# The last attention batch of a two-stage mixture-of-experts kernel: its chunk and transposes before the first ranks, two copies before a tile's root, and filler products in one batch instead of four

## The chip, the core and the metric

The kernel runs on one core of a Trainium2 chip. The core has TensorE (PE, the matrix engine, with its weight load PEld), VectorE (DVE), ScalarE (ACT), GpSimd (POOL) and SyncE (SP, which here only issues transfers), each with its own queue worked off in order. The metric is the device time of one execution in microseconds (us); less is better.

## What is computed

Attention without softmax (the keys' and values' 64x64 product per head, then the queries times it, then a root-mean-square norm), then two mixtures of eight experts, in which each token goes to the expert of its largest gate logit:

```
kv  = einsum('bhsd,bhse->bhde', k, v);  out = einsum('bhsd,bhde->bhse', q, kv)
x   = out / sqrt(mean(out*out) + 1e-6) * g_norm          # 4 batches, 8 heads, 576 x 64
# mixture 1: tokens with x @ w_skip > 0 only; e = argmax(x @ w_gate)
y   = gate_w * (relu(x @ w1[e]) @ w2[e]);  x = x + y     # D = 512, F = 1024, E = 8
# mixture 2: the same with other weights, at most 'capacity' tokens an expert; out = gate_w * y
```

There are 2304 tokens, so 18 tiles of 128.

## The kernel before

**Batches and tiles.** The attention goes through four batches of 576 tokens. A batch's `emit_kv` (line 698) multiplies keys and values in five chunks, `c0` to `c4`, into one PSUM tile, `acc`; after `c4` ScalarE copies the result to `vk` (two copies, lines 701 and 702). `emit_kvT` (`T` in the order) transposes it on TensorE into PSUM tile `lg` (line 710), multiplies it with the gates' weights into `acc` (line 713), and ScalarE copies both to `kvbd` (lines 715 and 716). Ahead of the transposes stand two filler products on zeros, `warm` (line 111), which compute nothing that is used. From `kvbd` come a tile's products `ops` (line 732). A tile then goes: ScalarE's square `sq` (741), VectorE's sum `ss` (743), ScalarE's copy `og` (749) and root `rm` (751), VectorE's `ri` (753), `lh` (757) and `Lall` (759, the gates' logits), a small copy of them (760), GpSimd's two products (764; in place on `og`, then into `xr`), and a store of `xr` to `xcat` (SP). `ops` has three buffers of two PSUM banks, `og` three buffers, so that tile 16's copy `og` waits for GpSimd's last product of tile 13.

**Ranks.** Routing needs each token's rank among those of its expert. It is done in two halves: tiles 0 to 8 while the attention still runs, tiles 9 to 17 after it. For the first half VectorE chooses the experts (`choose1`: `sel` at line 676, lines 153 to 161) and sums along them (`C`, line 173); TensorE makes the ranks in PSUM tile `lg` (`R` in the order: lines 178 and 183); VectorE reads them (`rk`, 196 and 198), splits them (`hb`, `hb`, `a`: 200, 202, 204) and builds one selection matrix `As` a tile (218, nine of them) and `Bt` (214). With `e` (line 785) the largest expert is found (`lead_1l`, 533, `order_1l`, 239, which SP reads before it loads that expert's weights). `E` is nine products with `As` (796), from which VectorE makes the indices `gi` (544 to 273), with which GpSimd gathers the rows of the first expert's first 128 tokens (`gather`, line 339). GpSimd's products of the tiles from 13 on are put behind this gather.

**After the attention** TensorE transposes the gathered rows (574), does half of the first layer for them (592), then the second half's ranks (again 178 to 183, which wait for `sel` and `C` of tiles 9 to 17), and so on through both mixtures.

**What sets the order.** On TensorE the order is the one in which the code is written, by the strings in `ATT_SEQ` (one for each batch: `t` a tile's products and its work, `c` a chunk of the next batch, `T` the next batch's transposes, `r`, `R`, `e`, `E` the ranks, `m`, `p` a tile's products and its work apart, `w` a load of weights, `q` the rest of the queries). On the other engines a scheduler orders by priority; ranks have a late one, and what stands under `high_priority` an early one. `behind(a, b)` puts instruction a after b. Lines are those of the kernel before; in the changed kernel a line past 708 stands four further down.

Of the kernel before, what the change touches and what calls it, by code (L numbers as in the profile page):

```python
# [12 lines left out]
AF = mybir.ActivationFunctionType  # L13
# [5 lines left out]
T = B * S  # L19
NT = T // 128  # L20
D = H * HD
E = 8
# [10 lines left out]
LPOOL = 16  # L33
G_DVE = (15,)
EARLY_SEQ = "v7 t v3 h0 h1 R h2 h3 T y0 y1"
ATT_SEQ = ["t0 c0 c1 t1 t2 c2 c3 c4 t3 T", "t0 c0 c1 t1 t2 c2 c3 c4 t3 T t4", "r t0 q c0 c1 t1 t2 c2 c3 R c4 t3 T", "e m0 m1 E w w p0 p1 t2 w w t3 t4"]
KV_COL = True
SPLIT1 = (1, 2, 3, 4, 5)
AS_POOL = 0
# [8 lines left out]
def moe_kernel(ctx: ExitStack, tc: tile.TileContext, qT, kk, vv, aux, w1a, w2a, w1b, w2b, capacity, out):  # L48
# [588 lines left out]
    with att:  # L637
# [48 lines left out]
        def emit_kv(b, cs_):  # L686

            vk = vk_all[b % 2]
            if 0 in cs_:
                kvp[b] = p1u.tile([128, 4, 128], F32, name="acc")  # L690
            ps = kvp[b]
            (k0, k1), (v0, v1) = kt[b], vt[b]
            for c in cs_:
                for hp in range(4):
                    for o, w in (((0, 64), (64, 64)) if KV_COL else ((0, 128),)):
                        cs = slice(hp * 128 + o, hp * 128 + o + w)
                        l, r = (v0[:, c, cs], k0[:, c, cs]) if c < 4 else (v1[:, cs], k1[:, cs])
                        nc.tensor.matmul(ps[o:o + w, hp, o:o + w], lhsT=l, rhs=r, start=(c == 0 and hp == 0), stop=(c == 4), skip_group_check=True)
            if 4 in cs_:
                with tc.high_priority():  # L700
                    nc.scalar.copy(out=vk[0:64, :, 0:64], in_=ps[0:64, :, 0:64])
                    nc.scalar.copy(out=vk[64:128, :, 64:128], in_=ps[64:128, :, 64:128])

        def emit_kvT(b):

            vk, kb = vk_all[b % 2], kvbd_all[b % 2]
            tp = p1u.tile([128, 4, 128], F32, name="lg")
            warm(tp, WARM_T)
            for hp in range(4):
                nc.tensor.transpose(tp[:, hp, :], vk[:, hp, :], ident)  # L710
            wp = p1u.tile([128, 4, 128], F32, name="acc")
            for hp in range(4):
                nc.tensor.matmul(wp[:, hp, 0:34], lhsT=vk[:, hp, :], rhs=gw[:, hp, :], start=True, stop=True)
            with tc.high_priority():
                nc.scalar.copy(out=kb[:, :, 0:128], in_=tp)
                nc.scalar.copy(out=kb[:, :, 128:162], in_=wp[:, :, 0:34])

        PS = {}

        def emit_products(i):  # L720
            t0 = i * 128
# [14 lines left out]
        def emit_tile(i):  # L736
            if i not in PS:
                emit_products(i)
            ps, t0 = PS[i], i * 128
            sq = asp.tile([128, 4, 128], F32, name="sq")  # L740
            nc.scalar.activation(out=sq, in_=ps[:, :, 0:128], func=AF.Square)
            ss = asp.tile([128, H], F32, name="ss")
            nc.vector.tensor_reduce(out=ss, in_=sq.rearrange("p c (h d) -> p (c h) d", h=2), axis=AX.X, op=ALU.add)
            og = asp.tile([128, H, HD], F32, name="og")
            o4, og4 = ps[:, :, 0:128].rearrange("p c (h d) -> p c h d", h=2), og.rearrange("p (c h) d -> p c h d", c=4)
            if i in G_DVE:
                nc.vector.tensor_tensor(out=og4, in0=o4, in1=grep.unsqueeze(1).unsqueeze(1).to_broadcast([128, 4, 2, HD]), op=ALU.mult)
            else:
                nc.scalar.copy(out=og4, in_=o4)
            rm = asp.tile([128, H], F32, name="rm")  # L750
            nc.scalar.activation(out=rm, in_=ss, func=AF.Sqrt, bias=eps6, scale=1.0 / HD)
            ri = asp.tile([128, H], F32, name="ri")
            nc.vector.reciprocal(out=ri, in_=rm)
            xr = axp.tile([128, ROW], F32, name="xr")
            r4 = ri.rearrange("p (c h) -> p c h", c=4).unsqueeze(3)
            lh = asp.tile([128, 4, 2, 17], F32, name="lh")
            nc.vector.tensor_tensor(out=lh, in0=ps[:, :, 128:162].rearrange("p c (h n) -> p c h n", h=2),
                                    in1=r4.to_broadcast([128, 4, 2, 17]), op=ALU.mult)
            nc.vector.tensor_reduce(out=Lall[:, i, :], in_=lh.rearrange("p c h n -> p n (c h)"), axis=AX.X, op=ALU.add)
            (nc.gpsimd.tensor_copy if i >= LPOOL else nc.scalar.copy)(out=xr[:, D:ROW], in_=Lall[:, i, 0:16])  # L760
            steps = [] if i in G_DVE else [(og, grep.unsqueeze(1))]
            steps.append((xr[:, 0:D].rearrange("p (h d) -> p h d", h=H), ri.unsqueeze(2)))
            for k, (dst, by) in enumerate(steps):
                ins = nc.gpsimd.tensor_tensor(out=dst, in0=og, in1=by.to_broadcast([128, H, HD]), op=ALU.mult)
                if "gather" in ahead and k == 0:
                    behind(ins, ahead["gather"])
            nc.sync.dma_start(out=xcat[t0:t0 + 128, :], in_=xr)
# [659 lines left out]
```

## Time and profile before

| | |
|---|---|
| median of 3 runs | 498.15 us (496.34 to 498.86) |
| the profiled execution | 496.94 us, of which its span 495.3 us |
| TensorE busy | 472.5 us (95%) |
| VectorE, ScalarE, GpSimd busy | 303.4, 205.8, 146.0 us |
| TensorE's mean granted clock | 0.982 of 2.4 GHz |
| chain that ended last, by engine | PE 83%, DVE 8%, DMA 3%, ACT 2%, issue 2%, POOL 1% |

The span is the profile's, from the first to the last instruction; what lies around it (1.6 us) is in the time alone. A granted clock of 1.00 is the level of 2.4 GHz, 0.50 that of 1.2 GHz. The attention takes some 68 us of the span; from about 75 us on the chain runs almost only along TensorE.

### The profile page before, as it was taken

Reading aid. Unit: us, or ns where it says so; the run is one execution under the profiler, and the core shown is the slowest. Engines: PE = TensorE matmul, PEld = TensorE weight load, DVE = VectorE, ACT = ScalarE, POOL = GpSimd, SP = SyncE. Lnnn points to the kernel's source line nnn. Section 1 sums busy time; section 2 is a strip of 40 time slices with the busy share of each in tenths; the row PEclk is TensorE's granted clock in tenths of the full one; section 3 lists DMA queues with packets and bytes.
Section 4 is the critical chain, followed back from the end, with each engine's and each line's share of the span. In section 5 each row is a group of like instructions: output and inputs, shape, how many; then the busy total and the mean of one; then the engine's idle time right before and its main releaser. Section 6 shows DMA issues by size and latency. Waiting matters only on the chain.

```text
span 495.3 us, 10239 instructions
## 1 busy us (share of the span) xinstructions
PE 472.5 (95%) x3824; PEld 450.7 (91%) x3829; DVE 303.4 (61%) x945; ACT 205.8 (42%) x524; POOL 146.0 (29%) x179
## 2 busy tenths in 40 slices
PE   6998778999999999999999999999999999999995
PEld 3897667999999999999998899999999999999984
DVE  2157978658767675265776576565657566675711
ACT  1376551344433532114233364454545545555400
POOL 5288584203021131113025230240604124040201
PEclk8599999999999999999999999999999999999999
DMA  8999495999768676358218993564656556400001
GB/s 236 362 356 347 163 355 154 315 323 348 269 229 299 206 290 210 126 194 314 91 45 304 414 336 142 193 202 150 214 187 221 201 179 215 144 37 2 35 23 41
DMA packets 24617, 104.90 MB, mean 212 GB/s; under 512 B 3609, under 2 KB 4761, under 8 KB 15984
## 3 DMA queue, kind: packets, MB, share of 16 engines
q1 hardware_dynamic: 17264, 77.75, 45.6%
q0 software_dynamic: 7008, 26.35, 15.1%
q8 instruction: 32, 0.52, 0.4%
q14 instruction: 25, 0.20, 0.1%
q10 hardware_dynamic: 288, 0.07, 0.1%
HBM read 92.15 MB, written 12.76 MB: 212 GB/s over the span
## 4 chain that ended last, share of the span: by engine, by line
PE 83%; DVE 8%; DMA 3%; ACT 2%; issue 2%; POOL 1%; SPq 0%; POOLq 0%; DVEq 0%; ACTq 0%
PE hp L592 14%; PE yp L1089 8%; PE yp L1091 8%; PE yp L1090 7%; PE hp L1089 6%; PE hp L1090 6%; PE hp L1091 6%; PE yp L626 6%; PE yp L616 6%; PE yp L617 2%; PE tp L1276 2%; PE yt L1320 2%; PE ops L732 2%; PE tp L1011 1%; PE tp L574 1%
## 5 line engine op out<-in xcount | busy, mean ns | idle before, releaser
L979 ACT CAST whi<-wraw 128x512 fp32r<-128x512 f32 x152 | 86.1, 619 | 73.3 <-PE yp L1090 30.1
L980 DVE TENSOR_TENSOR wlo<-wraw,whi 128x512 fp32r<-128x512 f32 x152 | 97.4, 684 | 26.1 <-ACT whi L979 25.0
L339 POOL DMA_INDIRECT rows<-xcat,gi x40 | 41.7, 1042 | 135.8 <-ACT ex L348 85.3
L1089 PE MATMUL hp<-xh,whi 128*128 128x256 f32 (+7 forms) x256 | 78.8, 308 | 0.2 <-DVE hl L1109 0.2
L592 PE MATMUL hp<-xT,wraw 128*128 128x128 f32 (+8 forms) x576 | 78.1, 292 | 0.5 <-ACT xT L576 0.5
L1091 PE MATMUL hp<-xh,wlo 128*128 128x256 f32 (+7 forms) x256 | 76.7, 299 | 0.0
L1090 PE MATMUL hp<-xl,whi 128*128 128x256 f32 (+7 forms) x256 | 76.6, 299 | 0.0
L592 PEld LDWEIGHTS hp<-xT,wraw 128*128 128x128 f32 x576 | 73.4, 190 | 2.9 <-issue 1.8
L1310 POOL DMA_INDIRECT out<-ot,toki x24 | 35.2, 1466 | 83.5 <-DVE su L352 39.5
L1089 PE MATMUL yp<-hh,whi 128*128 128x320 f32 (+5 forms) x192 | 58.8, 306 | 0.0
L1090 PE MATMUL yp<-hl,whi 128*128 128x320 f32 (+5 forms) x192 | 57.3, 298 | 0.0
L1091 PE MATMUL yp<-hh,wlo 128*128 128x320 f32 (+5 forms) x192 | 57.2, 298 | 0.0
L1089 PEld LDWEIGHTS hp<-xh,whi 128*128 128x128 f32 x256 | 48.3, 189 | 0.8 <-DVE hl L1109 0.5
L1090 PEld LDWEIGHTS hp<-xl,whi 128*128 128x128 f32 x256 | 48.3, 189 | 0.0
L1091 PEld LDWEIGHTS hp<-xh,wlo 128*128 128x128 f32 x256 | 48.3, 189 | 0.0
L1027 POOL DMA_INDIRECT xcat<-rows,toki x16 | 16.4, 1026 | 95.5 <-DVE mxt L297 93.1
L616 PE MATMUL yp<-hT,whi 128*128 128x352 f32 (+4 forms) x160 | 43.1, 351 | 0.0
L1108 ACT ACTIVATE hh<-hp 128x320 fp32r<-128x320 f32 (+8 forms) x64 | 27.2, 429 | 31.7 <-PE hp L1091 24.1
L1109 DVE SCALAR_TENSOR_TENSOR hl<-hp,hh 128x320 fp32r<-128x320 f32 (+8 forms) x64 | 30.0, 475 | 13.4 <-ACT hh L1108 12.8
L617 PE MATMUL yp<-hT,wlo 128*128 128x176 f32 (+4 forms) x160 | 37.7, 235 | 0.0
L1090 PEld LDWEIGHTS yp<-hl,whi 128*128 128x128 f32 x192 | 36.2, 189 | 0.0
L1089 PEld LDWEIGHTS yp<-hh,whi 128*128 128x128 f32 x192 | 36.2, 188 | 0.0
(255 smaller groups left out, 867.2 us busy)
## 6 DMA issues: line engine op xcount, KB each, us to landing
wraw<-in_w1a SPq DMA_DIRECT2D x14, 1024.0 KB
wraw<-in_w2a SPq DMA_DIRECT2D x14, 1024.0 KB, 5.6
wraw<-in_w1b SPq DMA_DIRECT2D x14, 1024.0 KB
wraw<-in_w2b SPq DMA_DIRECT2D x14, 1024.0 KB, 5.2
xcat<-xr SPq DMA_DIRECT2D x18, 264.0 KB, 3.9
q<-in_q SPq DMA_DIRECT2D x3, 1152.0 KB
wraw<-in_k SPq DMA_DIRECT2D x6, 512.0 KB, 10.2
wraw<-in_v SPq DMA_DIRECT2D x6, 512.0 KB, 12.8
```

What stands on the lines that cost most here:

```text
L339: return nc.gpsimd.indirect_dma_start(out=rows[:n], out_offset=None, in_=xcat[0:source], in_offset=bass.IndirectOffsetOnAxis(ap=gi[:n], ax ...
L592: nc.tensor.matmul(hp[:, ff, :], lhsT=wv[:, fc % 4, k, :], rhs=XT[j][:, k, c0:c1], start=(k == 0), stop=(k == 3))
L616: nc.tensor.matmul(yp, lhsT=wh[:, fc, :], rhs=HT[j][:, fc], start=(fc == 0), stop=False, skip_group_check=True)
L617: nc.tensor.matmul(yp[:, 0, :], lhsT=wl[:, fc, :], rhs=HT[j][:, fc, 0, :], start=False, stop=(fc == 7), skip_group_check=True)
L626: nc.tensor.matmul(yp[:, dd, :], lhsT=wv[:, dd, fc, :], rhs=HT[j][:, fc, c0:c1], start=(fc == 0), stop=(fc == 7))
L979: nc.scalar.copy(out=hi[:, cs], in_=raw[:, cs])
L980: ins = nc.vector.tensor_tensor(out=lo[:, cs], in0=raw[:, cs], in1=hi[:, cs].bitcast(F32), op=ALU.subtract)
L1089: nc.tensor.matmul(ps, lhsT=wh, rhs=xh, start=first, stop=False)
L1090: nc.tensor.matmul(ps, lhsT=wh, rhs=xl, start=False, stop=False)
L1091: nc.tensor.matmul(ps, lhsT=wl, rhs=xh, start=False, stop=last)
L1109: ev = nc.vector.scalar_tensor_tensor(out=hl[:, fs, cs], in0=hp, scalar=0.0, in1=hh[:, fs, cs].bitcast(F32), op0=ALU.max, op1=ALU.subtract)
L1310: st = nc.gpsimd.indirect_dma_start(out=out, out_offset=bass.IndirectOffsetOnAxis(ap=r2["toki"][:nn, j, bi:bi + 1], axis=0), in_=ot[:nn], ...
```

## The change

Three edits. In the third batch's string the ranks' products `R` move from ahead of `c4` to the string's end, behind the last batch's transposes `T`. In the last batch's `emit_kv`, the root `rm` of the tile emitted last (tile 11) is put behind the two copies to `vk`. And `emit_kvT` keeps its two filler products in the first batch alone.

```diff
-"r t0 q c0 c1 t1 t2 c2 c3 R c4 t3 T"
+"r t0 q c0 c1 t1 t2 c2 c3 c4 t3 T R"
...
-                    nc.scalar.copy(out=vk[64:128, :, 64:128], in_=ps[64:128, :, 64:128])
+                    ins = nc.scalar.copy(out=vk[64:128, :, 64:128], in_=ps[64:128, :, 64:128])
+                if b == B - 1:
+
+                    behind(RM[0], ins)
...
-            warm(tp, WARM_T)
+            if b == 0:
+                warm(tp, WARM_T)
...
-            nc.scalar.activation(out=rm, in_=ss, func=AF.Sqrt, bias=eps6, scale=1.0 / HD)
+            RM[0] = nc.scalar.activation(out=rm, in_=ss, func=AF.Sqrt, bias=eps6, scale=1.0 / HD)
```

TensorE, from the end of chunk `c3` of the last batch to the end of `T`, before:

```order
L178 LDWEIGHTS ones
L178 MATMUL lg<-C_0_656,ones 128x72
L183 LDWEIGHTS ntri
L183 MATMUL lg<-oh_0_646,ntri 128x72
L698 MATMUL acc<-k_249,v_250 64x64 x8
L732 MATMUL ops<-kvbd_196,q_245 128x162 x4
L111 LDWEIGHTS zb
L111 MATMUL lg<-zb 128x512
L111 LDWEIGHTS zb
L111 MATMUL lg<-zb 128x512
L710 MATMUL lg<-ident,vk_200 128x128 x4
L713 MATMUL acc<-gw,vk_200 128x34 x4
```

The same place now, with `e` (L789) and the first products of tile 13 behind it:

```order
L698 MATMUL acc<-k_249,v_250 64x64 x8
L736 MATMUL ops<-kvbd_196,q_245 128x162 x4
L714 MATMUL lg<-ident,vk_200 128x128 x4
L717 MATMUL acc<-gw,vk_200 128x34 x4
L178 LDWEIGHTS ones
L178 MATMUL lg<-C_0_652,ones 128x72
L183 LDWEIGHTS ntri
L183 MATMUL lg<-oh_0_642,ntri 128x72
L789 LDWEIGHTS ones
L789 MATMUL lg<-C_0_652,ones 128x8
L736 MATMUL ops<-kvbd_196,q_245 64x162 x4
L736 MATMUL ops<-kvbd_199,q_257 64x162 x4
```

The ranks and `e` now stand together between the transposes and tile 13; chunk `c4` and tile 12 follow chunk `c3` at once.

ScalarE, from the root of tile 10 to the copies to `kvbd` of the last batch, before:

```order
L751 ACTIVATE rm<-ss,eps_123 128x8
L749 COPY og<-ops 128x512
L751 ACTIVATE rm<-ss,eps_123 128x8
L701 COPY vk_200<-acc 64x4x64
L702 COPY vk_200<-acc 64x4x64
L760 COPY xr<-Lall 128x16 x2
L741 ACTIVATE sq<-ops 128x512
L749 COPY og<-ops 128x512
L715 COPY kvbd_199<-lg 128x4x128
L716 COPY kvbd_199<-acc 128x4x34
```

And now:

```order
L755 ACTIVATE rm<-ss,eps_123 128x8
L753 COPY og<-ops 128x512
L701 COPY vk_200<-acc 64x4x64
L702 COPY vk_200<-acc 64x4x64
L764 COPY xr<-Lall 128x16
L755 ACTIVATE rm<-ss,eps_123 128x8
L745 ACTIVATE sq<-ops 128x512
L719 COPY kvbd_199<-lg 128x4x128
L720 COPY kvbd_199<-acc 128x4x34
L764 COPY xr<-Lall 128x16
L753 COPY og<-ops 128x512
```

The copies to `vk` pass the root of tile 11, not that of tile 10; the copies to `kvbd` pass the copy `og` of tile 12.

VectorE, from the ranks' split `a` to the first steps for the largest expert, before (`ss` here is that of tile 12):

```order
L204 SCALAR_TENSOR_TENSOR a_0_771<-hb_0_768,rk_0_766 128x9
L207 SCALAR_TENSOR_TENSOR os_0_773<-hb_0_768,pi_88 128x18 x2
L218 TENSOR_SCALAR As<-rowb,a_0_771 128x128
L214 TENSOR_TENSOR Bt_202<-oh_0_646,os_0_773 128x288
L743 TENSOR_REDUCE ss<-sq 128x8
L218 TENSOR_SCALAR As<-rowb,a_0_771 128x128 x3
L529 TENSOR_TENSOR key_1l<-lg,sev 128x8
```

And now, from `Bt` to the last `As` (`ss` is that of tile 14; that of tile 13 stands just ahead of these rows):

```order
L214 TENSOR_TENSOR Bt_202<-oh_0_642,os_0_814 128x288
L218 TENSOR_SCALAR As<-rowb,a_0_812 128x128
L747 TENSOR_REDUCE ss<-sq 128x8
L757 RECIPROCAL ri<-rm 128x8
L218 TENSOR_SCALAR As<-rowb,a_0_812 128x128
L761 TENSOR_TENSOR lh<-ops,ri 128x136
L757 RECIPROCAL ri<-rm 128x8
L763 TENSOR_REDUCE Lall<-lh 128x17
L761 TENSOR_TENSOR lh<-ops,ri 128x136
L218 TENSOR_SCALAR As<-rowb,a_0_812 128x128
L763 TENSOR_REDUCE Lall<-lh 128x17
L218 TENSOR_SCALAR As<-rowb,a_0_812 128x128 x6
```

Behind the last row comes `lt` (line 544). Tile 12's `ss` stands ahead of the ranks' `rk` now, and eight of the nine `As` stand behind the `ss` of tile 14; before, all nine stood ahead of it.

On GpSimd the second load of the second expert's weights moves behind the branch for tokens beyond the slots (line 374).

## Rows read from the trace of the kernel before

**Rows 1.** Chain of waits, 26 to 75 us: start, length, engine, tile, line

```profile
61.36 1.29 POOL rows L339
...
62.67 2.50 POOL og L764 x2
...
69.61 3.19 DVE sel L676
...
74.54 0.32 DVE C L173
```

**Rows 2.** Timeline of TensorE: start, length, instructions, in brackets idle before

```profile
45.66 1.15 PE L698 MATMUL acc<-wraw 128*64 128x64 f32 x32
48.63 0.19 PE L178 MATMUL lg<-C,ones 128*128 128x72 bf16 x1 [1.82 <-DVE C L173]
...
49.40 1.37 PE L732 MATMUL ops<-kvbd,q 128*128 128x162 f32 x8
50.60 0.38 PE L111 MATMUL lg<-zb 128*128 128x512 bf16 x1
51.03 0.60 PE L710 MATMUL lg<-ident,vk 128*128 128x128 f32 x4
51.47 0.98 PE L713 MATMUL acc<-gw,vk 128*128 128x34 f32 x8
...
53.39 3.23 PE L732 MATMUL ops<-kvbd,q 128*64 128x162 f32 x24
...
58.53 0.42 PE L796 MATMUL acc<-Bt,As 128*128 128x32 bf16 x2 [1.49 <-DVE As L218]
...
59.78 5.25 PE L732 MATMUL ops<-kvbd,q 128*128 128x162 f32 x24
...
69.25 3.81 PE L592 MATMUL hp<-xT,wraw 128*128 128x128 f32 x32
74.91 0.21 PE L178 MATMUL lg<-C,ones 128*128 128x72 bf16 x1 [1.85 <-DVE C L173]
```

**Rows 3.** Timeline of ScalarE around the copies to vk

```profile
49.19 0.30 ACT L751 ACTIVATE rm<-ss,eps 128x8 f32<-128x8 f32 x1 [1.93 <-DVE ss L743]
...
50.43 0.37 ACT L702 COPY vk<-acc 64x256 f32<-64x256 f32 x1
```

**Rows 4.** Timeline of VectorE, first ranks to the indices

```profile
48.49 1.25 DVE L743 TENSOR_REDUCE ss<-sq 128x8 f32<-128x512 f32 x2
...
49.77 0.18 DVE L196 TENSOR_TENSOR rk<-lg,oh 128x72 f32<-128x72 f32 x1
...
51.32 1.02 DVE L200 TENSOR_SCALAR hb<-rk 128x9 f32<-128x9 f32 x1
...
60.91 0.15 DVE L272 TENSOR_SCALAR gi<-tok 128x1 int32<-128x1 f32 x1
```

**Rows 5.** Timeline of VectorE, the same split in the second ranks

```profile
75.84 0.16 DVE L200 TENSOR_SCALAR hb<-rk 128x9 f32<-128x9 f32 x1
```

**Rows 6.** Busy times by stretch: stretch, length, engines, granted clock (PEclk), DMA

```profile
14.00:18.00 4.00, 3.64 (x15) 3.01 (x15) 0.00 (x0) 1.27 (x4) 0.00 (x0) 0.50 1.03 387
47.00:48.60 1.60, 0.00 (x0) 0.00 (x0) 1.46 (x6) 0.26 (x1) 0.40 (x3) 1.00 1.06 386
61.00:62.00 1.00, 1.00 (x5) 1.00 (x5) 0.97 (x5) 0.20 (x1) 0.64 (x1) 0.50 0.96 262
64.00:65.00 1.00, 1.00 (x6) 0.93 (x7) 0.97 (x4) 0.30 (x1) 1.00 (x1) 0.85 1.01 426
```

**Rows 7.** Timeline of TensorE in the first batch

```profile
14.52 1.09 PE L710 MATMUL lg<-ident,vk 128*128 128x128 f32 x4
15.40 1.76 PE L713 MATMUL acc<-gw,vk 128*128 128x34 f32 x8
17.52 2.53 PE L732 MATMUL ops<-kvbd,q 128*128 128x162 f32 x8 [0.36 <-ACT kvbd L716]
```

**Rows 8.** Timeline of GpSimd while VectorE has sel in hand

```profile
71.73 1.03 POOL L764 TENSOR_TENSOR xr<-og,ri 128x512 f32<-128x512 f32 x1
```

More of the change, by code (lines that the diff above doesn't have):

```diff
@@ L35 @@
 EARLY_SEQ = "v7 t v3 h0 h1 R h2 h3 T y0 y1"
-ATT_SEQ = ["t0 c0 c1 t1 t2 c2 c3 c4 t3 T", "t0 c0 c1 t1 t2 c2 c3 c4 t3 T t4", "r t0 q c0 c1 t1 t2 c2 c3 R c4 t3 T", "e m0 m1 E w w p0 p1 t2 w w t3 t4"]
+ATT_SEQ = ["t0 c0 c1 t1 t2 c2 c3 c4 t3 T", "t0 c0 c1 t1 t2 c2 c3 c4 t3 T t4", "r t0 q c0 c1 t1 t2 c2 c3 c4 t3 T R", "e m0 m1 E w w p0 p1 t2 w w t3 t4"]
 KV_COL = True
@@ L716, in emit_kvT @@
                 nc.scalar.copy(out=kb[:, :, 128:162], in_=wp[:, :, 0:34])
-        PS = {}
+        PS, RM = {}, {}
         def emit_products(i):
```

## The prediction

> **What bounds the kernel now.** The page's chain shares come first: 83% of the span lies on TensorE. The change touches none of that bulk; it works between 28 and 60 us. So the second view is the chain of waits from 26 to 75 us, followed back from the second ranks. It doesn't run along TensorE there. It runs through VectorE to the gather, which GpSimd issues at 61.36, through GpSimd's products behind the gather, then through `sel`, which VectorE holds from 69.61 for 3.19 us, to `C` at 74.54 [rows 1]. On TensorE the second ranks start at 74.91, after 1.85 us of idle time that ended with `C` [rows 2]. Behind them TensorE has work without a long pause to the end of the span, so what moves this start moves the end.
>
> From the gather to the second ranks is 74.91 - 61.36 = 13.55 us. The instructions in between are the same before and after, and GpSimd's products are as many. So the question is **when the gather starts**, and whether TensorE is at full clock when it is needed.
>
> Third, TensorE's own timeline: it idles 1.82 us before the first ranks at 48.63, because they wait for `C` [rows 2]. That is the wait that the move takes away. It is no wait of the chain: VectorE is busy in 1.46 of the 1.60 us from 47.0 to 48.6, and TensorE in none [rows 6].
>
> **The change, part by part, and its cost.**
>
> *Filler products.* In the last batch the pair stands from 50.60, and the transposes behind it start at 51.03: 0.43 us [rows 2]. The pairs of the second and third batches are the same instructions, so TensorE reaches the third batch's work up to 0.86 earlier. What the choosing keeps of that I put at 0.3, since tiles wait for ScalarE and VectorE too; the ends are 0 and 0.86.
>
> *TensorE's order.* Chunks `c2` and `c3` end at 46.81 [rows 2], or 46.0 with 0.86 off. Then `c4` (half of the 1.15 of two chunks, 0.6) and tile 12 (1.37) run at once, and TensorE is through at 47.9. The transposes wait for the copies to `vk`, which end at 50.80 [rows 3]. These stand behind tile 10's root, which itself waited 1.93 us for VectorE's `ss` [rows 3], and that `ss` (48.49 [rows 4]) stands behind the ranks' `C` on VectorE, as before. The change moves the copies past tile 11's root alone: at most the 0.30 of such a root [rows 3]. With the 0.3 from above I put their end at 50.25. So TensorE's wait isn't removed but moved: from 47.9 to 50.3, **2.4 us**, in place of the 1.82.
>
> *First ranks at full clock.* The transposes and the product behind them take 51.47 + 0.98 - 51.03 = 1.42 [rows 2], so the ranks come at 51.75 in place of 48.63, and VectorE's `rk` at 52.0 in place of 49.77 [rows 4]: +2.2. Behind the ranks on TensorE stands `e`, which overwrites what `rk` reads, and behind `e` tile 13; I start tile 13 at 52.5, against 53.39 [rows 2].
>
> *VectorE from `rk` to the indices.* Before, `hb`, `hb` and `a` each ran beside a GpSimd product and took about a microsecond (the first 1.02 [rows 4]; there are three); without GpSimd beside it one takes 0.16 [rows 5]. Now only `lead_1l` meets a product, as it did before: 3 x 0.86 = -2.6. Tile 12's `ss` stands ahead of `rk`: -0.6 (half of the 1.25 for two [rows 4]). The short steps of tiles 13 and 14, partly behind the indices before, all stand ahead of them: between 0 and 1.25 (one `ss` for each set of three, as the nearest row); I take 0.8. Two waits for roots of tiles 12 and 14 are new, between 0 and the 0.9 by which a root waits and runs less its overlap; I take 0.4. Sum: 2.2 - 2.6 - 0.6 + 0.8 + 0.4 = **+0.2**. The ends are -0.9 (all fillers gained and no waits) and +1.2 (`lead_1l` held for a second product, 1.03 [rows 8]).
>
> *TensorE's clock.* The idle stretch of 1.82 us left the granted clock at 1.00 (47.0 to 48.6 [rows 6]). After the stretch from 57.0 to 59.8, in which TensorE waited 1.49 and then had a few short products [rows 2], it was 0.50 from 61.0 to 62.0 [rows 6]. The new idle stretch, 2.4 us, with 1.4 us of transposes and another wait of 0.8 behind it, resembles the second more than the first; no filler stands in it. I take it that the clock falls to 0.50 there. At 0.50 (14 to 18 us [rows 6]) the transposes and their product take 15.40 + 1.76 - 14.52 = 2.64, and a tile 2.53 against 1.37, 1.85 times as long [rows 7]. Tile 13 then starts at 53.2. Tiles 13 and 14 took 3.23 together [rows 2]; at half clock 6.0. In the run of tiles 15 to 17, from 59.78 [rows 2], the clock came back during 64.0 to 65.0 (mean 0.85 [rows 6], so at 64.3). I take as much of the run of tiles 13 and 14 at half clock, 4.5 us: they do 4.5 / 1.85 = 2.4 of the 3.23, the rest takes 0.8, and tile 14 ends at 53.2 + 4.5 + 0.8 = 58.5 in place of 52.5 + 3.2 = 55.7: 2.8 later.
>
> This matters because of VectorE's new order: eight of the nine `As` stand behind tile 14's `ss`, so they wait for tile 14's products; before, all nine stood ahead of it. VectorE would reach that `ss` about 0.7 after tile 14's square in the case at full clock, so of the 2.8 about **2.1** is left. Ends: 1.1 (the clock falls late or returns early) and 3.2 (all six microseconds at half clock).
>
> *Edits that cost nothing.* SP's loads of the first expert's weights wait for `order_1l`, which now comes ahead of the `As`; they start earlier, but nothing reads them before the gathered rows are transposed. GpSimd's second load of the next expert's weights goes behind a branch; it is first read more than 15 us later. If that cover were gone it would cost one issue, about the gather's 1.29 [rows 1].
>
> **Sum.** +0.2 + 2.1 = +2.3 on the gather, and as much on the second ranks and the end. Against the profiled execution's own 496.94 (span 495.3 and 1.6 around it) that is 499.2. The median of the runs is 1.2 above the profiled one, and I forecast a median: 498.15 + 2.3 = **500.4**.
>
> **Rivals.**
>
> *The clock holds.* The idle stretch is only 0.6 longer than the one that left it at 1.00 [rows 2, 6]. Then +0.2: 498.3. For it: the stretch may be cut if the copies come sooner. Against: what follows is sparse as well.
>
> *`sel` gets in sooner.* `sel` took 3.19 us from 69.61 and ended when GpSimd's last large product did (71.73 + 1.03 = 72.76 [rows 1, 8]), though three such products ended or began in that time. The `hb` of the first ranks waited for a single product and was through in 1.02 [rows 4]. If `sel` now meets GpSimd's series at another point and waits for one product, it ends 2.2 earlier; TensorE's own work (the first layer, 69.25 + 3.81 = 73.06 [rows 2]) then bounds the second ranks, so the gain is the idle 1.85. With the clock fallen 498.15 + 2.3 - 1.85 = 498.6, with the clock kept 496.5, under the half per cent either way. The Trainium skill, page "SBUF — State Buffer", section "Who interferes with whom", says that a VectorE instruction that needs the port pair shared with GpSimd blocks until the other's instruction has finished, and no longer; by that rule `sel` gets in at the first product's end. The row of `hb` agrees with it, the row of `sel` doesn't.
>
> *Clearly slower: the clock stays low up to the first layer.* Tiles 15 to 17 come later and in a sparser stretch; if the clock is still 0.50 when the first expert's first layer runs, its 3.81 us [rows 2] become 7.0 at 1.85 times. Less the 1.85 of idle time behind it, 1.4 is left, and with tiles 13 and 14 wholly at half clock (3.2) it is 0.2 + 3.2 + 1.4 = +4.8, 503.0. It decides from the point where the first layer starts before the clock is back at 1.00. Against it: seven fillers stand ahead of the first layer, and the gather's landing leaves time.
>
> **How the numbers follow.** A measurement of this kernel can tell about 0.5% (2.5 us) from no change. Chances: forecast 0.60, clock holds 0.18, `sel` sooner 0.10, clearly slower 0.12. The forecast's own ends, 0.2 + 1.1 and 0.2 + 3.2, straddle 2.5, a little more of it below: 0.35 of its 0.60 is "same", 0.25 slower. Same: 0.35 + 0.18 + 0.06 = 0.59, less 0.04 for errors of the sum; slower 0.25 + 0.12 + 0.02 = 0.39; faster 0.06, the `sel` rival with all the fillers' gain. The range: the clock-holds case less the runs' spread, 498.3 - 1.5 = 496.8, up to the forecast's upper end and some of the slower rival, 502.6.
>
> **What the changed profile would show.** Right: TensorE's transposes of the last batch at about 50.3 with over 2 us of idle time before them that end with a ScalarE copy; a granted clock of 0.50 within 50 to 58; tiles 13 and 14 taking over 4.5 us; six `As` in a row after 61; the gather at 63 to 64.5; the second ranks 13.5 later. Wrong: a gather before 62 (the clock held), `sel` under 1.5 us, or an idle stretch of TensorE before the second ranks that shrinks.

## The result, and the profile after

| | before | after |
|---|---|---|
| median, in one comparison of 20 runs each | 497.53 us (495.58 to 500.68) | 500.23 us (497.51 to 501.94) |
| ratio of the two, 95% interval | | 1.0051 (1.0034 to 1.0067) |
| profiled execution, its span | 496.94, 495.3 us | 500.29, 498.6 us |
| mean granted clock | 0.982 | 0.968 |

The change makes the kernel 0.5% slower, some 2.5 us by the ratio. The forecast was 500.4. The interval lies across the bound of 0.5% that the prediction drew between "same" and "slower".

TensorE's timeline after, from the last batch's transposes to the first layer's second half (start, length, instructions, in brackets the idle time before and what ended it), answers to [rows 2]:

```profile
50.59 1.11 PE L714 MATMUL lg<-ident,vk 128*128 128x128 f32 x4 [2.80 <-ACT vk L702]
51.50 1.76 PE L717 MATMUL acc<-gw,vk 128*128 128x34 f32 x8
53.07 0.25 PE L178 MATMUL lg<-C,ones 128*128 128x72 bf16 x1
...
53.81 4.90 PE L736 MATMUL ops<-kvbd,q 128*64 128x162 f32 x24
...
77.59 0.21 PE L178 MATMUL lg<-C,ones 128*128 128x72 bf16 x1 [1.94 <-DVE C L173]
...
78.33 5.23 PE L592 MATMUL hp<-xT,wraw 128*128 128x128 f32 x32
```

The idle time stands where the forecast put it: 2.80 us ahead of the transposes, ended by ScalarE's copy to `vk`, in place of the 1.82 ahead of the first ranks. Then the transposes take 1.11 in place of 0.60, the product behind them 1.76 in place of 0.98, tiles 13 and 14 4.90 in place of 3.23. The granted clock by stretches (stretch, length, TensorE's busy time and instructions, granted clock, DMA share, GB/s) says why; before, it was 1.00 in these:

```profile
47.00:50.00 3.00, 0.80 (x6) 1.00 0.82 272
50.00:53.00 3.00, 2.40 (x12) 0.60 0.77 259
53.00:56.00 3.00, 2.67 (x17) 0.50 0.48 180
...
77.00:80.00 3.00, 2.08 (x13) 0.65 0.82 238
```

On VectorE (answers to [rows 4]) the first ranks are read at 53.42 and six `As` stand in a row behind tile 14's `ss`:

```profile
48.21 0.31 DVE L173 TENSOR_TENSOR_SCAN C<-smask,oh 128x72 bf16<-128x72 f32 x1
...
53.42 0.23 DVE L196 TENSOR_TENSOR rk<-lg,oh 128x72 f32<-128x72 f32 x1 [0.63 <-PE lg L183]
...
54.58 0.95 DVE L533 TENSOR_SCALAR lead_1l<-key_1l,mx_1l 128x8 f32<-128x8 f32 x1
...
55.65 0.99 DVE L537 SCALAR_TENSOR_TENSOR bump_1l<-lack_1l,lead_1l 128x8 bf16<-128x8 f32 x1
...
59.44 0.69 DVE L747 TENSOR_REDUCE ss<-sq 128x8 f32<-128x512 f32 x1
...
61.62 1.05 DVE L218 TENSOR_SCALAR As<-rowb,a 128x128 bf16<-128x128 bf16 x6
...
72.36 3.13 DVE L676 TENSOR_SCALAR sel<-Lall 128x9 f32<-128x9 f32 x1
```

GpSimd issues the gather at 64.04, against 61.36 [rows 1]:

```profile
64.04 1.29 POOL L339 DMA_INDIRECT rows<-xcat,gi  x1 [7.42 <-DMA wraw<-in_w1a]
```

The row names a load of weights as what ended the wait. It is not what held the gather: the indices' last step ends at 63.80 (`toki`, 63.66 + 0.14), 0.24 us ahead of it, and before it is the same 0.24 (61.12 and 61.36).

From the gather to the second ranks it is 77.59 - 64.04 = 13.55 us, to the hundredth what it was before. The gather is 2.68 later, the second ranks are 2.68 later, the span is 3.3 longer. So 0.6 us of the difference lie behind the second ranks. There the first layer's second half (`h2`, `h3`) took 5.23 us, and 3.81 before, since the clock fell a third time (0.65 in 77 to 80); the rest of the span took 0.8 less than before.

**One correction to all starts.** The stage ahead of these rows doesn't end at the same time in every execution: VectorE's `C` of the first ranks starts at 48.27 before, 48.21 after, 46.98 in a second execution of the changed kernel. So below the gather is counted from that `C`: 61.36 - 48.27 = 13.09 before, 15.83 after. This hides little of what the fillers taken out ahead of `C` give: from the two chunks of keys and values ahead of the first of them (24.99 before, 25.05 after) `C` comes 23.28 and 23.16 us later. One run is an exception and is named there.

### The profile page after: what moved, and what is told of

Its sections match the earlier page's. It is cut to its first block, busy times and chain, and to the rows that moved or that the text cites. A ratio compares the mean times of both kernels' runs of the same rounds, so it can differ in the third digit from the quotient of the medians.

```text
span 498.6 us, 10239 instructions
## 1 busy us (share of the span) xinstructions
PE 476.7 (96%) x3823; PEld 454.4 (91%) x3823; DVE 304.4 (61%) x945; ACT 205.4 (41%) x524; POOL 143.1 (29%) x179
## 4 chain that ended last, share of the span: by engine, by line
PE 77%; DVE 2%; DMA 1%; ACT 0%; issue 0%; POOL 0%; POOLq 0%; ACTq 0%
PE hp L592 14%; PE yp L1093 7%; PE yp L1095 7%; PE yp L1094 7%; PE hp L1093 7%; PE hp L1094 6%; PE hp L1095 6%; PE yp L616 6%; PE yp L626 5%; PE yp L617 2%; PE tp L1280 2%; PE yt L1324 2%; PE tp L1015 1%; PE tp L574 1%; DMA rows<-xcat,gi 1%; PE lg L1002 1%
## 5 line engine op out<-in xcount | busy, mean ns | idle before, releaser
L592 PE MATMUL hp<-xT,wraw 128*128 128x128 f32 (+8 forms) x576 | 79.5, 295 | 0.8 <-ACT xT L580 0.5
L592 PEld LDWEIGHTS hp<-xT,wraw 128*128 128x128 f32 x576 | 74.8, 194 | 3.3 <-issue 1.8
L1314 POOL DMA_INDIRECT out<-ot,toki x24 | 32.8, 1368 | 83.9 <-DVE su L352 39.8
```

What stands on the lines that cost most here:

```text
L592: nc.tensor.matmul(hp[:, ff, :], lhsT=wv[:, fc % 4, k, :], rhs=XT[j][:, k, c0:c1], start=(k == 0), stop=(k == 3))
L1314: st = nc.gpsimd.indirect_dma_start(out=out, out_offset=bass.IndirectOffsetOnAxis(ap=r2["toki"][:nn, j, bi:bi + 1], axis=0), in_=ot[:nn], ...
```

## The experiments

There are three theories. **Theory 1**, the prediction's, is that the clock falls in the moved idle time, and that eight `As` behind tile 14's `ss` pass that on to the gather. **Theory 2** is that the ranks behind the transposes are late by themselves, whatever the clock. **Theory 3** is that it is the fillers that are missed.

Each ratio is against runs of the kernel before on the same chip in the same session; 0.001 is half a microsecond. The three columns behind are of the one profiled execution of each kernel, so they need not agree with the ratio, which comes from all its runs. "`As` early" means all nine `As` ahead of tile 13's `ss`. Line numbers shift by a few from kernel to kernel.

| kernel | ratio, 95% interval | gather less `C` | second ranks less gather | `h2`, `h3` |
|---|---|---|---|---|
| before | | 13.09 | 13.55 | 3.81 |
| after | 1.0051 (1.0034 to 1.0067) | 15.83 | 13.55 | 5.23 |
| after, a second execution | one run, 499.53 us | 15.50 | 13.56 | 3.81 |
| before + order on TensorE alone | 1.0067 (1.0044 to 1.0091) | 15.60 | 13.56 | 5.44 |
| before + fillers in one batch alone | 1.0056 (1.0036 to 1.0076) | 14.60 | 13.55 | 3.81 |
| after + 12 fillers | 1.0121 (1.0097 to 1.0146) | 17.80 | 13.56 | 5.44 |
| after + 12 fillers, order held | 1.0065 (1.0027 to 1.0103) | 14.50 | 13.55 | 5.43 |
| after + copies ahead of both roots | 1.0040 (1.0018 to 1.0063) | 14.01 | 13.55 | 5.44 |
| after + `As` early | 1.0011 (0.9985 to 1.0037) | 13.45 | 14.12 | 3.81 |
| before + `As` early | 1.0019 (0.9990 to 1.0048) | 13.51 | 13.55 | 3.81 |
| one batch's fillers, `As` early | 0.9991 (0.9969 to 1.0012) | 12.73 | 15.04 | 3.81 |
| the same + 15 more fillers later | 0.9981 (0.9960 to 1.0001) | 12.63 | 13.55 | 3.81 |
| after + copies, `As` early, 17 more fillers later | 0.9970 (0.9950 to 0.9989) | 11.97 | 13.55 | 3.81 |
| after + 9 fillers ahead of second ranks | 1.0029 (1.0009 to 1.0049) | 15.61 | 13.61 | 3.81 |

### The order on TensorE alone

```diff
-"r t0 q c0 c1 t1 t2 c2 c3 R c4 t3 T"
+"r t0 q c0 c1 t1 t2 c2 c3 c4 t3 T R"
```

> The kernel before with nothing changed but the order on TensorE: chunk and transposes ahead of the first ranks. Two fillers stay ahead of each batch's transposes, and ScalarE's copies are not held ahead of a tile's root by hand. Theory 1: TensorE still waits for the copies from about 47.8 to 50.3; two fillers of 0.3 us at the wait's end do not cover it, the clock falls to 0.50 at 50 to 51, tiles 13 and 14 take over 4.5 us, the gather starts at 63.0 to 64.5, and the time is 1.5 to 3.5 us above the kernel before. Theory 2: rk at 52.5 to 54, gather 63 to 64.5 and the same total, but without any need of a low clock. Theory 3: the clock stays at 1.00 and the gather is at 61 to 62; time within 0.8 us of the kernel before.

Measured: the gather came at `C` + 15.60, and the ratio is 1.0067, as large a loss as the whole change. The transposes waited 1.68 us behind the two fillers, the clock fell only after them (0.76 in 53 to 56), and tiles 13 and 14 took 4.83. So this one edit is enough for the loss, and fillers at the old place don't prevent it.

### The fillers alone

```diff
-            warm(tp, WARM_T)
+            if b == 0:
+                warm(tp, WARM_T)
```

> The kernel before with nothing changed but the fillers, which stay in the first batch alone. First ranks, chunk and transposes keep their places. Theories 1 and 2: the idle time ahead of the transposes is the copies' wait as before (about 2.0 us, split by the ranks), the clock stays at 1.00 from 47 to 58, the gather starts at 60.8 to 61.8, and the time is within 0.8 us of the kernel before. Theory 3: the clock falls to 0.50 in this stretch or earlier (24 to 48), tiles 13 and 14 take over 4.5 us, the gather starts after 62.5, and the time is 1.5 to 3 us above the kernel before.

Measured: the ratio is 1.0056, which theories 1 and 2 did not allow, and the mechanism of theory 3 wasn't there either: tiles 13 and 14 took 3.23 us at full clock. VectorE's timeline shows what was there (three of the nine `As` stand ahead of these rows):

```profile
58.54 0.23 DVE L218 TENSOR_SCALAR As<-rowb,a 128x128 bf16<-128x128 bf16 x1
...
58.76 0.66 DVE L744 TENSOR_REDUCE ss<-sq 128x8 f32<-128x512 f32 x1
59.35 0.56 DVE L218 TENSOR_SCALAR As<-rowb,a 128x128 bf16<-128x128 bf16 x3
59.84 0.67 DVE L744 TENSOR_REDUCE ss<-sq 128x8 f32<-128x512 f32 x1
...
60.54 0.19 DVE L218 TENSOR_SCALAR As<-rowb,a 128x128 bf16<-128x128 bf16 x1
...
61.55 0.25 DVE L218 TENSOR_SCALAR As<-rowb,a 128x128 bf16<-128x128 bf16 x1
...
62.10 0.17 DVE L544 TENSOR_TENSOR lt<-acc,lead_1l 128x16 f32<-128x16 f32 x1
```

In the kernel before, seven of the nine stood ahead of tile 13's `ss`, and the last two ahead of tile 14's:

```profile
58.70 0.66 DVE L743 TENSOR_REDUCE ss<-sq 128x8 f32<-128x512 f32 x1
59.29 0.39 DVE L218 TENSOR_SCALAR As<-rowb,a 128x128 bf16<-128x128 bf16 x2
59.62 0.67 DVE L743 TENSOR_REDUCE ss<-sq 128x8 f32<-128x512 f32 x1
```

The scheduler had moved the `As`. Here four stand ahead of tile 13's `ss`, three between the two, and the last two behind tile 14's, mixed with the work of that tile. The indices (`lt`, at 60.21 before) follow at 62.10. Six fillers that TensorE no longer runs (two in each of three batches) cost 1.5 us on the gather, counted from `C`, through another engine's order.

This is the run in which `C` itself was late: it came 24.51 us behind the two chunks named above (at 24.05 here), 1.2 more than before, after TensorE had waited 0.35 and 0.19 us for loads of values, and 0.97 us more with no cause in the profile, between 33 and 38 us. No other run without these fillers shows it (23.13 to 23.27), so it is likely to belong to this execution; one profile can't tell.

### Fillers in the moved idle time

```diff
             if b == 0:
                 warm(tp, WARM_T)
+            elif b == B - 1:
+                warm(tp, 12)
```

> The changed kernel with twelve filler products put back ahead of the last batch's transposes, so that TensorE is busy in the 2.8 us in which it now waits for ScalarE's copies. The instruction order changes with it on VectorE: the ranks' rk stands behind tile 12's logits, and five of the nine As stand ahead of ss(14). Theory 1 (the clock that falls in the moved idle time, with the As behind the late tile 14): the granted clock stays at 1.00 from 48 to 58, tiles 13 and 14 take 3.0 to 3.4 us instead of 4.90, the gather starts at 60.8 to 62.2, and the time is 2 to 3 us below the changed kernel, that is within 1 us of the kernel before. Theory 2 (the first ranks behind the transposes are late whatever the clock does): the clock holds just as well, but rk is at 53.0 to 54.0 as now, the gather at 63.5 to 64.5, and the time stays at about 500. Theory 3 (the fillers taken away are themselves what was missed): as theory 1 in the total, but with the clock at 1.00 in the changed kernel's place only if fillers stand there, so this run does not tell 1 from 3; the run that takes the fillers alone away does.

Measured: the gather came at `C` + 17.80, the ratio is 1.0121, and every theory missed. The idle time ahead of the transposes fell to 0.21 us, but a new one of 2.94 appeared behind them. ScalarE's timeline:

```profile
54.38 0.20 ACT L766 COPY xr<-Lall 128x16 f32<-128x16 f32 x1 [1.16 <-DVE Lall L765]
54.49 0.58 ACT L721 COPY kvbd<-lg 128x512 f32<-128x512 f32 x1
```

The scheduler had put the copies to `kvbd` behind tile 12's `og`, root and `xr`, which waits 1.16 for `Lall`. And on TensorE the ranks waited for the first of these copies:

```profile
55.12 0.22 PE L178 MATMUL lg<-C,ones 128*128 128x72 bf16 x1 [2.94 <-ACT kvbd L721]
...
55.83 5.61 PE L738 MATMUL ops<-kvbd,q 128*64 128x162 f32 x24
```

The reason is a tile of PSUM: the transposes, the ranks and `e` all write `lg`, of which there is one buffer. A product that is put behind the transposes there waits until ScalarE has emptied what they wrote. The clock then fell behind the transposes instead of ahead of them (tiles 13 and 14: 5.61).

So the trial was made again with VectorE's and ScalarE's order held near the changed kernel's (only the lines that set the order are shown; `PIN` and `r1['pin']` keep single instructions under a name):

```diff
+                behind(PIN['og12'], PIN['kv'])
+                behind(PIN['rm12'], PIN['kv'])
...
+                        behind(PIN['ri12'], r1['pin']['rk0'])
...
+            for k in range(1, 9):
+                behind(r1['pin'][f'as{k}'], PIN['ss14'])
```

> The changed kernel with twelve filler products ahead of the last batch's transposes, and VectorE's and ScalarE's instructions held in the changed kernel's order (eight As behind ss(14), the copies of the transposed product ahead of tile 12's og and root), which the first trial with fillers did not do. What is left of the difference is TensorE's clock. Theory 1: the clock is 1.00 from 48 to 57, tiles 13 and 14 take 3.0 to 3.4 us and end at 56 to 57.5, the gather starts at 61.0 to 62.7, 1.3 to 3 us ahead of 64.04, and the time falls by as much. Rival (the lower clock does no harm, the order of VectorE alone decides): tiles 13 and 14 end sooner but the gather stays at 63.3 to 64.3, and the time within 0.7 us of the changed kernel. If the transposed product's copies come over 1 us later than 51.74, as in the first trial, the clock falls again and nothing is told.

Measured: the clock was 1.00 from 47 to 59, and the gather came at 62.50, `C` + 14.50. TensorE's timeline:

```profile
50.39 0.66 PE L714 MATMUL lg<-ident,vk 128*128 128x128 f32 x4
...
52.76 0.19 PE L178 MATMUL lg<-C,ones 128*128 128x72 bf16 x1 [0.90 <-ACT kvbd L719]
...
53.41 3.23 PE L739 MATMUL ops<-kvbd,q 128*64 128x162 f32 x24
```

So the lower clock costs the gather 15.83 - 14.50 = 1.3 us (1.0 by the second execution of the changed kernel), and the other half of the loss, 14.50 - 13.09 = 1.4, stands at full clock. The ranks again wait for `lg`, 0.90 us. One `xr` copy stands ahead of the copies to `kvbd` here that doesn't in the changed kernel, and it waits 0.54 us for VectorE. The copy out of `lg` starts at 52.13 behind it; without it, it could have started behind `sq`, at about 51.5. So up to half a microsecond of the 1.4 belongs to this run's order, and the clock's share may be as much more. The ratio, 1.0065, did not fall with the gather; in the profiled execution `h2` and `h3` took 5.43 (see the third fall, below), and with five runs of this kernel in the comparison the interval is too wide to say more.

### The copies ahead of both roots

```diff
-                    behind(RM[0], ins)
+                    behind(RM[10], ins)
+                    behind(RM[11], ins)
...
-            RM[0] = nc.scalar.activation(out=rm, in_=ss, func=AF.Sqrt, bias=eps6, scale=1.0 / HD)
+            RM[i] = nc.scalar.activation(out=rm, in_=ss, func=AF.Sqrt, bias=eps6, scale=1.0 / HD)
```

> The changed kernel with both ScalarE copies of the last batch put ahead of the roots of tiles 10 and 11 (now the copies still stand behind tile 10's root, which waits 1.92 us for VectorE). The As stay behind ss(14). Theory 1: the copies are done at 47.5 to 48.5, the transposes start at 47.9 to 48.7 with under 1 us of idle time ahead, the clock stays at 1.00 to 58, tiles 13 and 14 take 3.0 to 3.4 us and end at 54 to 55.5, the gather starts at 59.5 to 61.3, and the time is 0 to 2 us below the kernel before. Theory 2: rk is at 50.5 to 52 since only the transposes stand ahead, a gather at 61 to 62.5 and a time within 1 us of the kernel before even if the clock falls. If the clock falls all the same (0.50 in 50 to 58): tiles 13 and 14 take 4.9 us and the gather comes at 62 to 63.

Measured: the transposes start at 47.84 with 0.50 us idle ahead, as expected, but the gather came at `C` + 14.01, and the clock fell all the same, from 53 on:

```profile
47.84 0.66 PE L715 MATMUL lg<-ident,vk 128*128 128x128 f32 x4 [0.50 <-ACT vk L702]
...
50.65 0.19 PE L178 MATMUL lg<-C,ones 128*128 128x72 bf16 x1 [1.34 <-ACT kvbd L720]
...
51.68 4.86 PE L737 MATMUL ops<-kvbd,q 128*64 128x162 f32 x24
```

The ranks wait 1.34 us for `lg`, since the copies to `kvbd` now stand behind the two roots. Taking one wait away let the next one in. Ahead of the fall TensorE had waited 0.50, 1.34 and 0.70 us; the clock was at 0.50 from 53 to 56.

### All `As` ahead of tile 13's `ss`

```diff
-                        late(lambda: run(gen))
+                        run(gen)
```

This lifts the late priority of the first ranks' work on VectorE. In the changed kernel:

> The changed kernel with one priority altered: the first ranks' work on VectorE is no longer put off behind later work, so that all nine As stand ahead of ss(13) instead of eight behind ss(14). TensorE's and ScalarE's order up to there stays. Theory 1 (the loss is As standing behind a tile 14 that is late): the clock still falls at about 50.5, tiles 13 and 14 still take 4.9 us and end at 58.7, yet the nine products of As follow them at once and end by 60.0, the gather starts at 60.5 to 62.0 against 64.04, and the time is 1.5 to 3 us below the changed kernel. Theory 2 (the later ranks cost by themselves): rk stays at 53.4 and the gather at 63 to 64.5. If the clock at 78 to 81 is an effect of chance it may or may not fall there: 1.4 us either way.

TensorE, VectorE and GpSimd:

```profile
52.87 4.59 PE L736 MATMUL ops<-kvbd,q 128*64 128x162 f32 x24
57.30 0.95 PE L800 MATMUL acc<-Bt,As 128*128 128x32 bf16 x9
...
69.83 5.16 PE L592 MATMUL hp<-xT,wraw 128*128 128x128 f32 x32
```

```profile
56.61 1.38 DVE L218 TENSOR_SCALAR As<-rowb,a 128x128 bf16<-128x128 bf16 x8
...
58.05 0.68 DVE L747 TENSOR_REDUCE ss<-sq 128x8 f32<-128x512 f32 x1
```

```profile
60.71 1.29 POOL L339 DMA_INDIRECT rows<-xcat,gi  x1 [5.04 <-DVE gi L272]
```

The clock fell as in the changed kernel (tiles 13 and 14: 4.59), and yet the gather came at `C` + 13.45, 2.0 to 2.4 earlier than in the changed kernel's two executions and 0.4 behind the kernel before; the ratio is 1.0011. The last `As` ends at 57.99, behind tile 14's products (57.46), so here the last of the nine products waits for VectorE and not for the slow tiles. That is theory 1's second half, and the larger: **where the `As` stand decides, and the fall of the clock reaches the gather almost only through `As` that wait for tile 14.** Theory 2 alone does not explain the loss, since `rk` is as late here as after (`C` + 5.21). The edit moves more than the `As`: the split (`hb`, `hb`, `a`, `os`) is done 0.6 us earlier too, ahead of `lead_1l`. The last `As` ends 3.7 us earlier (`C` + 10.73 against 14.46), so most of it is the `As`' own place.

In the kernel before, the same edit gives nothing; in the kernel with one batch's fillers it takes the loss back. First the kernel before:

> The kernel before with the same one priority altered: all nine As ahead of ss(13) (before: five or six ahead of it, the rest behind ss(13)). If the gather waits for the last As in the kernel before too, it moves from 61.36 to 58.5 to 60.0; of that the second ranks keep 0.5 to 2.5 us, since tiles 15 to 17 and GpSimd's products then bound them, and the time is 0.5 to 2.5 us below the kernel before. If the ranks on VectorE now delay the logits of tiles 13 and 14 by as much, the second ranks stay where they are and the time within 0.5 us.

Measured: the gather came at `C` + 13.51, and the ratio is 1.0019. (The expectation counts the `As` of before wrongly: seven stand ahead of tile 13's `ss`.) The gain on the last `As` goes to `bump_1l` and the `ss` of tiles 12 to 14, which now stand between them and the indices.

Then the kernel with one batch's fillers:

> The kernel before without fillers past the first batch, and with all nine As ahead of ss(13). Without fillers alone the gather came at 63.16 although the clock held to 58, with two As behind ss(14), tile by tile between other work. If the planner's new order of the As is what the fillers' removal cost (theory 1, second half), the gather comes at 58.5 to 61.0 and the time falls by 2 to 4 us against that run, to within 1 us of the kernel before or below it. If the removal costs by something else (clock, or the earlier batches), the gather stays after 62 and the time 2 to 3 us above the kernel before.

Measured: the gather came at `C` + 12.73 against 14.60, and the ratio is 0.9991. Of the earlier gather the second ranks saw little in the profiled execution, which at 497.97 us was 1.4 above the median of this kernel's runs: they came 15.04 behind it. TensorE waited 3.86 us for the gathered rows, and the first layer then took 4.48:

```profile
68.81 0.96 PE L574 MATMUL tp<-ident,rows 128*128 128x128 f32 x4 [3.86 <-DMA rows<-xcat,gi]
...
70.84 4.48 PE L592 MATMUL hp<-xT,wraw 128*128 128x128 f32 x32
75.15 0.20 PE L178 MATMUL lg<-C,ones 128*128 128x72 bf16 x1
```

With more fillers in that wait:

```diff
-EARLY_SEQ = "v7 t v3 h0 h1 R h2 h3 T y0 y1"
+EARLY_SEQ = "v22 t v3 h0 h1 R h2 h3 T y0 y1"
```

> The kernel before without fillers past the first batch and with all nine As ahead of ss(13), as run once already (gather at 60.11), plus 22 instead of 7 filler products while TensorE waits for the gathered rows. There TensorE stood idle 3.86 us ahead of the first layer's transposes, the clock fell, the two first-layer series took 4.48 us instead of 3.81, and the second ranks came 15.04 us after the gather instead of 13.55. If that wait is what ate the earlier gather (theory 1), the clock stays at 1.00 through 65 to 76, h0 and h1 take 3.8 us, the second ranks come 13.5 to 13.9 us after the gather, and the time is 1 to 2 us below the run without, 0.5 to 2.5 us below the kernel before. Rival: the second ranks are held by VectorE's sel behind GpSimd's products, which follow the gather in any case, and the first layer's clock is off the path: less than 0.5 us from the run without.

```profile
70.02 3.73 PE L592 MATMUL hp<-xT,wraw 128*128 128x128 f32 x32
73.59 0.21 PE L178 MATMUL lg<-C,ones 128*128 128x72 bf16 x1
```

Measured: the first layer is back at 3.73 us, and the second ranks are back at 13.55 behind the gather. The ratios, 0.9981 and 0.9991, can't be told apart.

### The three together

The copies ahead of both roots, the `As` early, and `v24`:

> The changed kernel with the copies ahead of both roots, with all nine As ahead of ss(13), and with 24 filler products ahead of the first layer: the three causes found taken away together. Theory 1: transposes at about 48, As done by 56.5, tiles 13 and 14 done by 56.5 even at the lower clock, the gather at 58 to 60 against 64.04, the second ranks 13.5 to 14.5 us after it, and the time 1 to 4 us below the kernel before. Rival: with the gather that early the tiles 15 to 17 and GpSimd's products are the bound, the second ranks stay at 74 to 75.5 and the time within 0.5 us of the kernel before.

```profile
51.30 4.85 PE L737 MATMUL ops<-kvbd,q 128*64 128x162 f32 x24
...
72.83 0.21 PE L178 MATMUL lg<-C,ones 128*128 128x72 bf16 x1 [0.78 <-DVE C L173]
```

The gather comes at `C` + 11.97, and at 0.9970 (0.9950 to 0.9989) this is the one kernel of the study whose interval lies below 1: about 1.5 us under the kernel before, some 4 under the changed one, compared through the kernel before (one comparison, not repeated). The expectation's other end, 4 us, is not reached; the clock still falls (tiles 13 and 14: 4.85).

### The third fall of the clock

> The changed kernel as it is, profiled once more. Theory 1: idle ahead of the transposes 2.6 to 3.0 us, the clock at 0.50 from about 50 to 57, tiles 13 and 14 at 4.5 to 5.0 us, the gather 15.5 to 16.1 us after VectorE's first C. Whether h2 and h3 take 5.2 us or 3.8 us again tells how far the third fall of the clock belongs to the kernel.

```profile
49.37 1.11 PE L714 MATMUL lg<-ident,vk 128*128 128x128 f32 x4 [2.79 <-ACT vk L702]
...
52.58 4.58 PE L736 MATMUL ops<-kvbd,q 128*64 128x162 f32 x24
...
76.78 3.81 PE L592 MATMUL hp<-xT,wraw 128*128 128x128 f32 x32
```

The second execution has everything of the first but the third fall: `h2` and `h3` take 3.81. Then the wait ahead of them was filled in the changed kernel (`v9` ahead of `R` in `EARLY_SEQ`):

> The changed kernel with nine filler products ahead of the second ranks, in the 1.94 us in which TensorE waits for VectorE's C; up to there the order on the engines is the changed kernel's (one weight load of GpSimd's queue is issued a little sooner after it). If the third fall of the clock (77.85 to 81.3, h2 and h3 at 5.23 us instead of 3.81) comes from that idle time and belongs to most executions of the changed kernel: clock 1.00 from 72 to 84, h2 and h3 at 3.8 us, and the time 1.0 to 1.6 us below the changed kernel. If the fall is an accident of the one execution: time within 0.5 us of the changed kernel's. The fillers can hold the ranks by 0.2 us where C comes before they end.

Measured: the clock was 1.00 from 68 to 86, `h2` and `h3` took 3.81, and the ratio is 1.0029 (1.0009 to 1.0049) beside the changed kernel's 1.0051 (1.0034 to 1.0067). The difference is about 1.1 us, as the theory of a common fall wants, but the intervals overlap; it isn't settled. Over all profiles: in eight the idle time ahead of the second ranks was 1.84 to 1.95 us, and the clock fell behind it in five of them; in the other six it was at most 0.83 us, and it fell in none. From the second ranks to the span's end the five with the fall took 421.0 to 422.8 us, the nine without 419.4 to 421.9: 1.4 longer on average, which is what `h2` and `h3` lose, with ranges that overlap.

## Why the prediction was right, and where only its sum was

**The time.** The forecast was 500.4, and 500.23 was measured; the sum on the gather was +2.3 against +2.68 (from `C`, 2.74 and 2.41 in the two executions). That the totals agree to 0.2 us is in part luck. Two terms of the sum were wrong in opposite directions, the third fall of the clock stands in none, and the median from which the forecast starts (498.15, of three runs) is 0.6 above that of the comparison (497.53).

**Right: the wait is moved, not removed.** The forecast was 2.4 us, and 2.80 was measured. The copies passed one root, and the rest of the ScalarE chain stayed. What was off is the fillers' 0.3: of it 0.1 arrived at `C` (23.16 us behind the earlier chunks in place of 23.28).

**Right: the clock falls there.** It was at 0.50 from about 50.6 to 57.4. The transposes and their product end 2.67 us after they start (2.64 forecast), and tiles 13 and 14 take 4.90 (5.3 forecast). It fell in all four executions with an idle time of 2.79 or 2.80 us ahead of the transposes. The rival "the clock holds" is out.

**Wrong: the sum at full clock, +0.2.** Counted from `C` this is +0.5, since the forecast has `C` itself 0.3 earlier. With the clock held, the loss is 1.4 as measured, and by estimate 0.9 or more without that run's `xr` copy. The failed step is "the ranks come at 51.75 in place of 48.63, and VectorE's `rk` at 52.0". It let the ranks follow the transposes' product at once. They write `lg`, the tile that the transposes have just written, and wait for ScalarE's copy: 0.90 us in the run with the clock held (up to 0.6 of it owed to the `xr` copy), 0.91 in the run with the order alone, 1.34 and 2.94 in others. `rk` stands at `C` + 5.02 with the clock held, and by the forecast it would have stood at about `C` + 4.0. The row that said so was there; it is of the kernel before and shows `e`, the next product into `lg` behind the transposes:

```profile
53.29 0.17 PE L785 MATMUL lg<-C,ones 128*128 128x8 bf16 x1 [0.84 <-ACT kvbd L715]
```

The prediction kept this as "another wait of 0.8" behind the transposes, but let the ranks, which take the same buffer, start without it. In the changed kernel itself the wait can't be seen, since the slower product behind the transposes covers it.

**Right: VectorE from `rk` to the indices.** The forecast at full clock was -2.0 (-2.6 - 0.6 + 0.8 + 0.4); from `rk` to `gi` it was 11.14 before and is 9.03 with the clock held (62.05 - 53.02). Two short steps met a GpSimd product, not one (`hb` 0.92 and `lead_1l` 1.00 there; `lead_1l` 0.95 and `bump_1l` 0.99 in the changed kernel). So the other terms together must have come out lower by about as much; no run takes them apart.

**Too large: the clock's price, 2.1.** The two runs that differ in it give 1.0 to 1.3, and by the `xr` copy named there up to half a microsecond more. One reason is a misread row. The prediction counts the stretch at half clock in tiles 15 to 17 from their start, 59.78, to 64.3, and gets 4.5 us. But in the kernel before the clock was still up when they started (the granted clock is the third number from the end):

```profile
60.00:61.00 1.00, 1.00 (x8) 0.97 (x8) 1.00 (x9) 0.47 (x2) 0.00 (x0) 0.95 0.31 57
```

A mean of 0.95 in 60 to 61 puts the fall at about 60.9, so the stretch was 3.4 us. With 3.4 the prediction's own sum gives 4.8 us for tiles 13 and 14 in place of 5.3; 4.58 to 4.90 were measured in four executions.

**Right: the conduit.** The price was said to come from eight `As` behind tile 14's `ss`. With the `As` ahead, and the clock as low, 2.0 to 2.4 of the loss is gone. So the order is more than a conduit: in the run without fillers, at a clock that held to 58, two `As` behind tile 14's `ss` go with 1.5 us.

**Right: from the gather on.** The 13.55 us are unchanged, and from the start of `sel` to `C` it is 4.87 us (4.93 before). The second ranks' `sel` took 3.12 to 3.19 in every profile here; it never got in at the end of a single product, so the rival "`sel` gets in sooner" is out. The rule of the Trainium skill ("SBUF — State Buffer", "Who interferes with whom"), by which whoever issues first holds the shared ports for its whole instruction and the other blocks, agrees with `hb`, `lead_1l` and `bump_1l` (0.92 to 1.02 each, to the end of one GpSimd product) and not with this `sel`, which waits through several; the rows decide. It does agree with the first ranks' `sel`, the same instruction (after the change):

```profile
42.54 2.50 POOL L768 TENSOR_TENSOR og<-og,au 128x512 f32<-128x512 f32 x2
45.00 2.04 POOL L768 TENSOR_TENSOR xr<-og,ri 128x512 f32<-128x512 f32 x2
```

```profile
43.79 1.28 DVE L676 TENSOR_SCALAR sel<-Lall 128x9 f32<-128x9 f32 x1
```

This one ends at 45.07, with the second `og` (45.04), though `xr` follows at once; in the other profiles it took 0.33 to 1.28 us. Why the second one is passed over stays open.

The 13.55 holds only while TensorE has no longer wait ahead of the first layer: it was 14.12 and 15.04 where that wait was 4.13 and 3.86 us and the first layer then ran at the lower clock (5.16 and 4.48).

**Not foreseen: the edits don't add.** The order on TensorE alone costs about 3.3 us, the fillers alone 2.8, all three edits together 2.5. The fillers were priced at what they take on TensorE; what the gather lost without them, 1.5 us, came from what the scheduler does with VectorE's order once they are gone. And the third fall, 1.42 us in the profiled execution, stands in no term; the "clearly slower" rival looked for it in the first layer's first half, not in its second.

## What to carry to other kernels

Before a product is moved, list who else writes its PSUM buffer: the wait for the reader of that buffer goes along with the place, not with the product. Where a scheduler sets the other engines' order, the price of removing an instruction is read from that order and not from the instruction's length. And when a wait turns out to be moved, ask which work stands behind the late engine for no reason of data: here taking nine short selections that didn't need the late tile out from behind it gave more on the gather (2.0 to 2.4 us) than holding the clock did (1.0 to 1.3).

## What the runs showed of the hardware

- The clock isn't the same in each execution of one order of instructions. Up to the first ranks three kernels share the order on TensorE without fillers; idle for 2.39 to 2.56 us there, the clock fell in two (tile 12 at 2.53 and 2.32 us) and held in one (1.37). Of two executions of the changed kernel one had the third fall (`h2` and `h3` at 5.23 us) and one had not (3.81). So a fall seen in a single profile is a sample.
- A single long wait isn't needed: in the run with the copies ahead of both roots TensorE waited 0.50, 1.34 and 0.70 us between 47 and 52, and the clock was at 0.50 from 53 to 56.
- Of a row of short VectorE steps none to four are held by GpSimd products, mostly for about a microsecond (0.88 to 1.19, against 0.15 without), and which ones they are changes with the order. The second ranks' `sel` (3.12 to 3.19) is held through a whole series, the first ranks' (at most 1.28) to the end of one product.
